# One block of a weight loaded ahead of k and v: a change of load order in a fused attention and MLP kernel

## Chip, cores, metric

The kernel runs on one NeuronCore of one Trainium2 chip. The metric is the device time of one execution in microseconds (us). Traces are of one execution each; "span" is from the first to the last instruction of the trace, 1.8 us less than the timed figure of the same execution. PE is TensorE (with its weight loads as PEld), DVE VectorE, ACT ScalarE, POOL GpSimd, SP SyncE; the results of the matmuls stand in tiles of PSUM pools, which DVE or ACT reads (in the trace of before ACT takes 1.02 us for each `rt<-hps`, DVE 0.76 us for two `qpTp<-tq`).

## The reference

Batch 8, 8 heads, 576 positions, head size 64, all in float32. Linear attention with cosine and sine features, then an MLP with a squared ReLU:

```python
k_p, q_p = phi(k, cos, sin), phi(q, cos, sin)   # relu(x) * cos, relu(x) * sin, side by side
kv  = einsum('bhsf,bhsd->bhfd', k_p, v);  z = k_p.sum(axis=2)
x   = (q_p @ kv) / ((q_p * z).sum(-1) + 1e-6)   # per head; reshaped to 4608 x 512
out = relu(x @ w_in)**2 @ w_out                 # w_in 512 x 2048, w_out 2048 x 512
```

## The kernel before

The weights are loaded once, cast to bf16 by the DMA, in four pieces each; a w_out block is four row groups of 128 rows (1 MB in float32; the page lists 512 KB for each of these loads). q, k and v are loaded per batch, as one main part and two tails. Batch 0 comes in on the SP queue. Everything here is issued by POOL (GpSimd):

```python
def load_w2(i, n):                       # block i of n of w_out
    h0, h1 = i * HB // n, (i + 1) * HB // n
    nc.gpsimd.dma_start(out=w2sb[:, h0:h1, :], in_=moe_w_out[h0 * P : h1 * P, :]...)

with tc.manual_schedule():
    load_batch(0, nc.sync, "kvq")
    ...                                  # constants, warm-up matmuls, features of k, v of batch 0
    for i in range(4):
        load_w1(i, 4)
    load_batch(1, nc.gpsimd, "qkv")      # the lines of the change
    for i in range(4):
        load_w2(i, 4)
    load_batch(2, nc.gpsimd, "qkv")
    att_kv(0, 0)
    ...                                  # attention of batch 0
    for s in range(len(slots)):
        run(s)
```

The work then goes through slots. Slots 0 to 7 are the first GEMM of batch 0, with parts of the attention of batches 0 and 1 between them; slots 8 to 15 are the second GEMM of batch 0. It is the first reader of w_out. It has four outputs at once: the two halves of one buffer of the PSUM pool `ps_h`, and the two buffers of `ps_y`. `ps_y` also holds the transposed q features:

```python
def gemm2(b, s):
    if b == 0:
        if s == 0:
            yh = ps_h.tile([P, 2, DM], F32, name="yh", tag="hps", bufs=2)
            ypss[b] = [yh[:, 0, :], yh[:, 1, :]]
            for i in range(2):
                yps = ps_y.tile([P, DM], F32, name="yps", tag="yps", bufs=2)
                ypss[b].append(yps[:, :])
        for hb in range(s * HB // 8, (s + 1) * HB // 8):     # two row groups per slot
            for tt in range(J):                              # four outputs
                gemm2_mm(b, tt, hb, ypss[b][tt])
```

The last transposes of q (`tq`, line 279) stand in slot 7 and are copied out by DVE (`qpTp`, line 288). The features of k and the copy of v of batch 1 stand in slots 8 and 9, and their product (`kz`, line 236) in slot 10.

## Time and profile before

Three runs took 300.75 to 301.13 us, median 301.09. Busy shares of the span: PE 97%, ACT 51%, DVE 46%, POOL 16%. PE (TensorE) is the engine to look at, and its only wait on w_out is the 1.27 us in front of the second GEMM of batch 0, the place that the change aims at. The lines for it are in the prediction.

### The profile page before, as it was taken

To read this page: it belongs to the slowest core of one execution; us is meant where nothing else is said; L and a number is where in the kernel's file an instruction comes from. 1 tells how busy PE (TensorE), PEld (TensorE's weight loads), DVE (VectorE), ACT (ScalarE), POOL (GpSimd) and SP (SyncE) were. 2 spreads that over 40 slices of the span, in tenths; PEclk is the share of its full clock that TensorE was granted. 3 is DMA by queue.
4 is the path that set the end of the run, shared out by engine and by line. 5 is a ranking of instruction groups with operands and counts; after the bars stand their busy time and mean duration, and the time that the engine had idled before them with its cause. 6 is when DMAs were issued, how large, how long until landed. Compare 5 with 4: busy or idle time off the path is not lost.

```text
span 299.0 us, 6477 instructions
## 1 busy us (share of the span) xinstructions
PE 291.1 (97%) x2701; PEld 202.3 (68%) x2701; DVE 136.6 (46%) x333; ACT 153.0 (51%) x213; POOL 47.8 (16%) x79
## 2 busy tenths in 40 slices
PE   8799989999999999999999999999999999999995
PEld 3379845889456984589654884589754894589544
DVE  2367654475648386228730287227740273024100
ACT  3465743666738554655554555555563552255311
POOL 1463404661121002000021001100021000100000
DMA  7999993999639987898568926898468115100021
GB/s 211 284 204 342 288 231 123 329 355 248 163 97 181 229 253 112 257 248 239 140 175 208 327 43 90 268 256 242 124 168 212 37 35 81 70 35 3 34 73 70
DMA packets 77069, 52.98 MB, mean 177 GB/s; under 512 B 52240, under 2 KB 71952, under 8 KB 77040
## 3 DMA queue, kind: packets, MB, share of 16 engines
q1 hardware_dynamic: 67120, 29.50, 42.2%
q0 software_dynamic: 9776, 22.94, 27.1%
q8 instruction: 21, 0.34, 0.5%
q10 hardware_dynamic: 144, 0.13, 0.1%
q14 instruction: 8, 0.07, 0.1%
HBM read 36.70 MB, written 9.44 MB: 154 GB/s over the span
## 4 chain that ended last, share of the span: by engine, by line
PE 86%; DMA 10%; POOL 1%; SPq 1%; issue 0%; ACT 0%; ACTq 0%
PE yps L413 40%; PE hps L378 38%; DMA q<-in_q_dram 5%; PE num L305 3%; DMA w2sb<-in_moe_w_out_dram 3%; DMA v<-in_v_dram 3%; PE kz L236 3%; PE yh L413 2%; POOL w1sb L117 1%; SPq L69 0%; PE tx L346 0%; PE tq L279 0%; POOL vt L69 0%; POOL vext L195 0%; SPq L64 0%
## 5 line engine op out<-in xcount | busy, mean ns | idle before, releaser
L378 PEld LDWEIGHTS <-w1sb 128*128 128x128 bf16 x1312 | 113.2, 98 | 12.1
L378 PE MATMUL hps<-xT,w1sb 128*128 128x256 bf16 (+1 forms) x1056 | 118.0, 269 | 0.0
L413 PE MATMUL yps<-w2sb,gT 128*128 128x512 bf16 (+1 forms) x496 | 110.4, 372 | 0.0
L386 ACT ACTIVATE rt<-hps 128x1024 bf16<-128x1024 f32 x72 | 73.7, 1024 | 59.2 <-DVE gT L393 32.8
L413 PEld LDWEIGHTS <-gT 128*128 128x128 bf16 x528 | 49.6, 98 | 54.0 <-DMA w2sb<-in_moe_w_out_dram 1.4
L393 DVE TENSOR_TENSOR gT<-rt 128x1024 bf16<-128x1024 bf16 x64 | 44.0, 688 | 82.8 <-ACT rt L386 82.8
L409 POOL DMA_DIRECT2D out_dram<-ysb x34 | 20.5, 605 | 176.2 <-ACT ysb L399 173.2
L399 ACT COPY ysb<-yps 128x512 f32<-128x512 f32 (+1 forms) x35 | 20.0, 575 | 55.3 <-PE yps L413 55.3
L181 ACT ACTIVATE qp<-q,sin_col 128x512 bf16<-128x512 f32 x32 | 21.9, 719 | 6.4 <-DMA q<-in_q_dram 6.4
L181 ACT ACTIVATE kp<-k,sin_col 128x512 bf16<-128x512 f32 x32 | 21.2, 714 | 3.1 <-DMA k<-in_k_dram 3.1
L319 DVE TENSOR_TENSOR x<-num,rden 128x512 bf16<-128x512 f32 x32 | 22.1, 691 | 1.1
L171 DVE TENSOR_SCALAR qp<-q,cos_col 128x512 bf16<-128x512 f32 x32 | 14.5, 492 | 11.7 <-DMA q<-in_q_dram 11.7
L315 DVE TENSOR_SCALAR den<-num 128x8 f32<-128x8 f32 (+1 forms) x40 | 6.6, 165 | 23.9 <-PE num L305 23.7
L171 DVE TENSOR_SCALAR kp<-k,cos_col 128x512 bf16<-128x512 f32 x32 | 15.1, 481 | 4.9 <-DMA k<-in_k_dram 4.9
L378 PE MATMUL hps<-xTt,w1sb 128*128 128x128 bf16 x256 | 15.3, 219 | 0.0
L413 PE MATMUL yps<-w2sb,gTt 128*128 128x512 bf16 x64 | 14.5, 379 | 0.0
L195 DVE CAST vext<-v 128x512 bf16<-128x512 f32 (+1 forms) x31 | 13.0, 425 | 2.9 <-DMA v<-in_v_dram 2.9
L305 PEld LDWEIGHTS <-qpT 128*128 128x128 bf16 (+1 forms) x240 | 10.3, 100 | 3.3 <-issue 1.7
L236 PEld LDWEIGHTS <-kp 128*128 128x128 bf16 x256 | 9.5, 97 | 4.4 <-issue 1.9
L201 PE MATMUL wm<-zeros 128*128 128x512 bf16 x42 | 10.9, 421 | 1.2 <-DVE zeros L86 1.2
L305 PE MATMUL num<-kvz,qpT 128*128 128x65 bf16 (+1 forms) x240 | 11.7, 194 | 0.0
L236 PE MATMUL kz<-vext,kp 128*128 128x65 bf16 x256 | 9.9, 193 | 1.6 <-DVE vext L195 1.6
(58 smaller groups left out, 132.6 us busy)
## 6 DMA issues: line engine op xcount, KB each, us to landing
out_dram<-ysb POOLq DMA_DIRECT2D x28, 256.0 KB, 3.9
k<-in_k_dram SPq DMA_DIRECT2D x5, 1024.0 KB, 6.2
v<-in_v_dram SPq DMA_DIRECT2D x5, 1024.0 KB, 6.7
q<-in_q_dram SPq DMA_DIRECT2D x5, 1024.0 KB, 5.9
q<-in_q_dram POOLq DMA_DIRECT2D x3, 1024.0 KB, 13.7
k<-in_k_dram POOLq DMA_DIRECT2D x3, 1024.0 KB, 10.1
v<-in_v_dram POOLq DMA_DIRECT2D x3, 1024.0 KB, 9.7
w1sb<-in_moe_w_in_dram POOLq DMA_DIRECT2D x4, 512.0 KB, 8.8
```

The lines of the kernel that those rows point to most:

```text
L171: nc.vector.tensor_scalar(out=dst[:, :, 0:D], in0=src, scalar1=0.0, scalar2=cos_col[:, j : j + 1], op0=ALU.max, op1=ALU.mult,)
L181: nc.scalar.activation(out=dst[:, :, D:F], in_=src, func=ACTF.Relu, scale=sin_col[:, j : j + 1])
L195: copy(out=vx[:, j, h0:h1, 0:D], in_=piece("v", b, j)[:, h0:h1, :])
L236: nc.tensor.matmul(out=kz[:, half, hh * E1 : (hh + 1) * E1], lhsT=lhsT, rhs=rhs, start=(j == 0 and hh == 0), stop=(j == J and hh == HH - 1),)
L305: nc.tensor.matmul(out=out, lhsT=lhsT, rhs=kvz[:, half * HH + hh, :], start=True, stop=True)
L319: nc.vector.tensor_tensor(out=x_of(b, j).rearrange("p (b k) (l d) -> p b k l d", b=n, l=2), in0=n4[:, :, :, 0:D].rearrange("p b (k l) d -> ...
L378: nc.tensor.matmul(out=out, lhsT=w1sb[:, kb, hb * P : (hb + 1) * P], rhs=rhs, start=(kb == 0), stop=(kb == KB - 1),)
L386: nc.scalar.activation(out=rt[:, :, :], in_=hps[:, :, :], func=ACTF.Relu)
L393: nc.vector.tensor_tensor(out=dst, in0=rt[:, :, :], in1=rt[:, :, :], op=ALU.mult)
L399: nc.scalar.copy(out=ysb[:, c0:c1], in_=acc)
L409: eng.dma_start(out=dst, in_=ysb[p0 : p0 + n, c0:c1])
L413: nc.tensor.matmul(out=acc, lhsT=lhsT, rhs=w2sb[:, hb, c0:c1], start=(hb == 0), stop=(hb == HB - 1))
```

## The change

The intent is to have the first block of w_out on the chip when PE first wants it, at the cost of k and v of batch 1, which are wanted later.

```diff
-        load_batch(1, nc.gpsimd, "qkv")
-        for i in range(4):
+        load_batch(1, nc.gpsimd, "q")
+        load_w2(0, 4)
+        load_batch(1, nc.gpsimd, "kv")
+        for i in range(1, 4):
             load_w2(i, 4)
```

## The prediction

> **What bounds the kernel now.** I read the page first, then the waits, the chain that ended last, and the order of time on each engine between 11 and 60 us. The page says that PE (TensorE) is the engine to look at:
>
> ```profile
> span 299.0 us, 6477 instructions
> PE 291.1 (97%) x2701; PEld 202.3 (68%) x2701; DVE 136.6 (46%) x333; ACT 153.0 (51%) x213; POOL 47.8 (16%) x79
> ```
>
> PE is idle for 299.0 - 291.1 = 7.9 us in the whole span. By the order of time on PE, 2.8 of it lie before 11.75 us, where the first matmuls on real data start, and 3.2 behind the last matmul at 295.8. A change in load order can win only what remains. The table of waits names that remainder; in each line the sum comes first, then how often, then the longest:
>
> ```profile
> PE kz L236 <- DVE vext L195: 1.6, 1, 1.6
> PEld L413 <- DMA w2sb<-in_moe_w_out_dram: 1.4, 1, 1.4
> PE yh L413 <- DMA w2sb<-in_moe_w_out_dram: 1.3, 1, 1.3
> ```
>
> The last two are one event, seen from the weight loads and from the matmuls. It is the only PE wait that involves w_out, and it happens once. The chain of waits shows where, and that PE works without a gap behind it:
>
> ```profile
> 14.87 13.74 DMA q<-in_q_dram
> 28.61 0.28 issue
> 28.89 0.61 POOL vt L69
> 29.50 8.73 DMA w2sb<-in_moe_w_out_dram
> 38.23 0.05 issue
> 38.27 0.60 PE yh L413 x2
> 38.88 0.43 PE yps L413 x2
> ```
>
> Columns: start, length, what. Block 0 of w_out is issued at 29.50 and lands at 38.23. From 38.27 until 295.78, just before the last copy, the chain is PE pieces alone. The order of time on PE gives the size:
>
> ```profile
> 36.40 0.61 PE L279 MATMUL tq<-ident,qp 128*128 128x128 bf16 x8
> 38.27 0.60 PE L413 MATMUL yh<-w2sb,gT 128*128 128x512 bf16 x2 [1.27 <-DMA w2sb<-in_moe_w_out_dram]
> ```
>
> PE ends the transposes at 37.01 (rounded; 38.27 - 1.27 = 37.00) and starts the second GEMM of batch 0 at 38.27. So 1.27 us, 0.4% of 301.09, is the ceiling of what this change can remove.
>
> [...] the loads issued on POOL (GpSimd) land in order of issue, q of batch 1 at 14.87 + 13.7 = 28.6, k at 17.27 + 15.1 = 32.4, v at 23.36 + 12.1 = 35.5, w_out block 0 at 38.2. [...]
>
> **The change, part by part.** Nothing is removed or added. The instruction lists of PE, DVE (VectorE), ACT (ScalarE) and SP are identical; on POOL the first w_out load moves up past six loads (k, two k tails, v, two v tails). Cost of issue: the same instructions, 0.76 us for a w_out block, 0.9 for a main load, 0.6 for a tail.
>
> *Issue waits.* POOL's order of time shows that it often waits before issuing:
>
> ```profile
> 20.84 0.62 POOL L69 DMA_DIRECT2D kt<-in_k_dram  x1 [2.02 <-DMA w1sb<-in_moe_w_in_dram]
> 23.36 0.90 POOL L64 DMA_DIRECT2D v<-in_v_dram  x1 [1.90 <-DMA w1sb<-in_moe_w_in_dram]
> 25.86 0.64 POOL L69 DMA_DIRECT2D vt<-in_v_dram  x1 [1.60 <-DMA w1sb<-in_moe_w_in_dram]
> 28.89 0.62 POOL L69 DMA_DIRECT2D vt<-in_v_dram  x1 [2.39 <-DMA q<-in_q_dram]
> ```
>
> The compiled list explains them: POOL's loads rotate through eight semaphores, so each waits for the load eight places earlier. The moved block becomes the eighth load and waits for nothing: it is issued behind the q tails, at 17.27 instead of 29.50. Each load of k and v inherits the wait of its new place: k at 18.0 (the first w_in piece lands at 11.73 + 6.1 = 17.8), its tails at 20.84 and 23.36, v at 25.86 and its tails at 28.6 and about 29.2. Block 1 goes out near 30, as now; block 2 waits for block 0, block 3 for k.
>
> *Landings.* Between v and block 0, and between blocks, the spacing is 38.2 - 35.5 = 2.7 and about 2.5 us (two issues starting at 29.50 and 30.26 have a median of 9.6 to landing; with 8.7 for the first, 10.5 for the second, so block 1 lands at 40.8). Block 0 should then land at 28.6 + 2.7 = 31.3, and k and v slip by one block, 2.5 us: k to 34.9, v to 38.0. Block 1 has the same bytes ahead of it as before and stays at 40.8; so do blocks 2 and 3. All are estimates from the trace's own spacings.
>
> *What k and v meet.* DVE and ACT don't take them up at once, as DVE's order of time shows:
>
> ```profile
> 37.04 0.76 DVE L288 COPY qpTp<-tq 128x512 bf16<-128x512 bf16 x2 [0.44 <-PE tq L279]
> 37.72 0.68 DVE L393 TENSOR_TENSOR gT<-rt 128x1024 bf16<-128x1024 bf16 x1
> 38.31 0.48 DVE L171 TENSOR_SCALAR kp<-k,cos_col 128x512 bf16<-128x512 f32 x1
> 38.71 0.42 DVE L195 CAST vext<-v 128x512 bf16<-128x512 f32 x1
> ...
> 41.50 0.30 DVE L193 CAST vextt<-vt 128x256 bf16<-128x256 f32 x1
> ```
>
> DVE first reads k at 38.31 (3.4 us after the new landing) and v at 38.71 (0.7 us after). ACT first reads k at 37.52. The reader on PE, the k-v product, runs at 43.46 now and near 42.5 when it moves up by 1 us; DVE has its last input ready at 41.80. That is 0.7 us of slack at its first matmul, more for v's tail, which only its last eight need. v may be about 0.7 + 0.7 = 1.4 us later than I estimate before PE stands still for it.
>
> *What PE gets.* Block 0 is in place 5.7 us before PE wants it, so PE starts at 37.01. Two smaller waits then come to light.
> First, the four outputs of that GEMM use two buffers each of two PSUM pools; the fourth takes the buffer of the transposes that PE has only just ended, which DVE copies out until 37.04 + 0.76 = 37.80. PE arrives at 37.01 + 3 x 0.216 = 37.66 (a pair of these matmuls takes 0.43). With the hand-over I count 0.2 us lost.
> Second, block 1 is first read after 16 matmuls. Three are done by then and 13 x 0.216 = 2.81 follow 37.85: PE is there at 40.66[...]. Before, it came at 41.90 (by the chain, 38.27 plus the first pieces), 1.1 us after block 1's landing; now it meets the landing at 40.8 almost exactly. Should block 1 land there, its matmuls start at 40.85.
> Sum: 41.90 - 40.85 = 1.05 us gained; I take off 0.1 for the chance that block 1 is a little later. Blocks 2 and 3 (issued by 35, needed near 46 and 50) land well ahead. All later work of the other engines follows PE's progress, and the DMA queue drains by about 49 us (18 GB/s between 47 and 50 us), so nothing should give the gain back. Predicted: 301.09 - 0.95 = 300.1 us.
>
> **Rivals.** *The wait moves to k and v.* They land later, and DVE works in order, so a late v would also hold its later k pieces. Needed for a loss: v at 39.4 or later. For it: the loads get their semaphores later (v's tail at 29.2 at the earliest). Against: the queue then still holds some 8 us of earlier bytes. If true, PE idles before the k-v product, by 0.5 to 2 us, and the time is 300.5 to 302.
> *The wait moves to block 1 of w_out.* Likely as a trace of a wait, since the times tie. If the reorder costs the queue 0.5 us, half the gain goes: 300.6. [...]
> *Everything is gained.* If the PSUM buffer is free in time and block 1 lands earlier, at 40.3: 1.2 us, 299.9.
> *Nothing is gained, since a later wait takes it back.* PE has no gap after 38.27 in the chain, but small slacks elsewhere may be used up. It would leave 301.1. I see no line that speaks for it.
>
> **Range and chances.** The three runs spread over 0.38 us, about a third of the effect. The gain can hardly exceed 1.27, and 0.3 is a plausible low; with 0.2 to 0.4 us of run-to-run shift, 299.5 to 300.8 should hold it 8 times in 10. Faster by 2% would need 6.0 us where 1.27 are to be had. Slower by 2% would need a 7 us stall; only a much later landing of v could do it.
>
> **What would show it.** Right: PE's wait on w_out at 37 us is gone or under 0.3; block 0 lands near 31, v near 38; a wait of 0.1 to 0.3 on the DVE copy in front of the fourth output; the k-v product of batch 1 starts near 42.5 without a wait on k, v or DVE; PE's idle time falls by about 1 us and its busy time stays at 291. Wrong: PE idle before the k-v product, a wait for block 1 over 0.4 us, or a new gap after 50 us.

41.90 - 40.85 = 1.05 us, less 0.1, gives the 0.95 us and the 300.1 us. The "8 us of earlier bytes" is an estimate from the 8.73 us that block 0, issued at 29.50, took to land. The eight semaphores are read from the compiled list; the four waits in its lines agree, each with the load eight places earlier (the last tail of v goes out at 28.89, after q of batch 1 has landed at 28.6).

## More of the kernel before

The granted clock is the share of its full speed that the profile records for PE, and a run's mean clock is its average over the span.

## The result, and the profile after

| | runs | median us | range us |
|---|---|---|---|
| before | 4 | 301.11 | 300.75 to 302.01 |
| changed | 4 | 299.52 | 299.38 to 299.65 |

The ratio is 0.9943, with an interval of 0.992 to 0.9965. (Ratios here are the mean time of one kernel's fast runs over that of the other's of the same rounds, so not quite the ratio of the medians.) The class "within 2%" was right. The gain was not: 1.6 us by the medians, 1.7 by the ratio, where 0.95 was predicted. The time lies on the lower edge of the stated range; by the ratio, 0.9943 x 301.09 = 299.4, it is outside.

The page of the changed kernel:

```profile
span 297.6 us, 6476 instructions
PE 292.3 (98%) x2701; PEld 202.5 (68%) x2701; DVE 136.5 (46%) x333; ACT 153.0 (51%) x213; POOL 47.8 (16%) x79
```

The span is 1.4 us shorter, yet PE is busy 1.2 us longer. That has nothing to do with the change: the 34 warm-up matmuls at the start took 8.96 us in the trace of before and 10.32 in this one, and a second trace of the kernel before also has 292.1. Busy time alone would mislead here.

PE's order of time, where the wait was (start, length, engine, line, what, count, idle before and its cause):

```profile
36.04 0.61 PE L279 MATMUL tq<-ident,qp 128*128 128x128 bf16 x8
36.49 0.59 PE L413 MATMUL yh<-w2sb,gT 128*128 128x512 bf16 x2
36.92 0.38 PE L413 MATMUL yps<-w2sb,gT 128*128 128x512 bf16 x1
37.50 0.39 PE L413 MATMUL yps<-w2sb,gT 128*128 128x512 bf16 x1 [0.20 <-DVE qpTp L288]
```

The wait on w_out is gone; the second GEMM starts as the transposes end, and the fourth matmul waits 0.20 us for the DVE copy that frees its buffer. DVE's order of time shows that copy, and that k and v are read without a wait:

```profile
36.69 0.76 DVE L288 COPY qpTp<-tq 128x512 bf16<-128x512 bf16 x2 [0.44 <-PE tq L279]
37.36 0.68 DVE L393 TENSOR_TENSOR gT<-rt 128x1024 bf16<-128x1024 bf16 x1
37.96 0.48 DVE L171 TENSOR_SCALAR kp<-k,cos_col 128x512 bf16<-128x512 f32 x1
38.35 0.42 DVE L195 CAST vext<-v 128x512 bf16<-128x512 f32 x1
```

The landings (issue on POOL plus time to landing, us):

| load | before: issued, landed | changed: issued, landed | predicted landing |
|---|---|---|---|
| q, batch 1 | 14.87, 28.6 | 14.52, 28.1 | 28.6 |
| w_out block 0 | 29.50, 38.2 | 16.91, 31.2 | 31.3 |
| k, batch 1 | 17.27, 32.4 | 17.66, 34.1 | 34.9 |
| v, batch 1 | 23.36, 35.5 | 25.37, 37.4 | 38.0 |
| w_out block 1 | 30.26, 40.8 | 29.64, 40.0 | 40.8 |

So where did 1.4 us of span come from? The fifth pair of `yh` matmuls, the first to read block 1, starts at 41.90 before and 40.48 after, 1.42 earlier (by the chain that ended last, as in the prediction; the order of time has both 0.17 earlier). Of this, 0.35 is older than the change: the trace of before has PE at the end of the transposes at 37.00, this one at 36.65, as all of it had begun earlier: q of *batch 0*, loaded by SP long before the moved load, was first used at 14.36 against 14.03. The other 1.07 is the removed wait less the new one, as predicted. In these two traces the mechanism gave its predicted size, and the timed runs showed 0.5 more.

### The profile page after: what moved, and what is told of

Same layout as the page of the kernel before. It is cut to its first block, busy times and chain, and to the rows that moved or that the text cites. A ratio compares the mean times of both kernels' runs of the same rounds, so it can differ in the third digit from the quotient of the medians.

```text
span 297.6 us, 6476 instructions
## 1 busy us (share of the span) xinstructions
PE 292.3 (98%) x2701; PEld 202.5 (68%) x2701; DVE 136.5 (46%) x333; ACT 153.0 (51%) x213; POOL 47.8 (16%) x79
## 3 DMA queue, kind: packets, MB, share of 16 engines
q1 hardware_dynamic: 67120, 29.50, 43.2%
## 4 chain that ended last, share of the span: by engine, by line
PE 93%; DMA 3%; SPq 1%; DVE 1%; ACT 0%; issue 0%; ACTq 0%
PE hps L378 43%; PE yps L413 40%; PE num L305 3%; DMA q<-in_q_dram 3%; PE kz L236 3%; PE yh L413 2%; PE tq L279 1%; SPq L69 1%; PE tx L346 1%; PE wm L209 1%; ACT qpTp L288 0%; SPq L64 0%; DVE qp L171 0%; DVE qpTp L288 0%; ACT ysb L399 0%
## 5 line engine op out<-in xcount | busy, mean ns | idle before, releaser
L201 PE MATMUL wm<-zeros 128*128 128x512 bf16 x42 | 12.2, 460 | 1.2 <-DVE zeros L86 1.2
L413 PEld LDWEIGHTS <-gTt 128*128 128x128 bf16 x64 | 6.3, 98 | 7.6
```

The source lines that it names most:

```text
L413: nc.tensor.matmul(out=acc, lhsT=lhsT, rhs=w2sb[:, hb, c0:c1], start=(hb == 0), stop=(hb == HB - 1))
```

## The experiments

Theory at first (A): the start varies from run to run, and the change is worth its 1.07 us. Rival (B): the changed program starts earlier as well, always. A third reading came out of the first session: (C) the wait itself is longer in most runs of the kernel before than in the trace that I read. Each session has its own chip; a session's first-named time of the kernel before is from runs taken between those of the tried kernels. By the 2% rule of the record all these kernels are "same", e8 "unclear"; the text goes by the ratios and their 95% intervals.

### Second session: the kernels again, and the 0.2 us wait

**e1**, the kernel before, unchanged.

> The kernel before, unchanged, as a control. Theory A (the extra 0.35 us at the start is run-to-run variation of the first loads): the first use of q of batch 0 on DVE, at 14.36 us in the first trace of this kernel, moves by some tenths between traces of one and the same kernel; PE waits 1.2 to 1.3 us for block 0 of w_out again; ratio to before 1.000 within 0.1%. Theory B (the start depends on the program): 14.3 to 14.4 us again, and 14.0 only in the changed kernel.

Measured: 301.3 us median of 6 (300.6 to 301.9), ratio 0.9999 (0.9973 to 1.0025). Its trace:

```profile
36.88 0.61 PE L279 MATMUL tq<-ident,qp 128*128 128x128 bf16 x8
39.38 0.60 PE L413 MATMUL yh<-w2sb,gT 128*128 128x512 bf16 x2 [1.89 <-DMA w2sb<-in_moe_w_out_dram]
```

The wait is 1.89 us, half as long again as in the first trace of the same program. The first use of q of batch 0 came at 14.88 (14.36 before): the start moves by half a microsecond in one program, which is enough for A to explain the 0.35. But I had expected the wait to stay at 1.2 to 1.3, and that failed.

**e2**, the changed kernel, unchanged.

> The changed kernel, unchanged. Theory A: the gain is only the wait for block 0 less the new 0.2 us wait, 1.07 us by the traces, so a ratio of 0.9964 and about 300.0 us where before takes 301.1. Theory B: the start is earlier with the changed program as well, 1.4 us, ratio 0.9953, with the first use of q at 14.0 us again. If the first ratio of 0.9943 (1.7 us) holds, more than the two terms that the traces show is in it and both theories lack something.

Measured: 299.81 us median of 6 (299.34 to 300.08) against 301.02 of 11 (300.45 to 302.9); ratio 0.9951 (0.9927 to 0.9974), 1.5 us. First use of q at 14.23. The fourth matmul waits 0.20 us again. The first matmul on block 1 starts at 40.62, 0.18 late, with block 1 landing at 40.6: the tie that the prediction saw, lost this time.

**e3**, the changed kernel with the first eight matmuls of the second GEMM in the order of outputs:

```diff
-        for hb in range(s * HB // 8, (s + 1) * HB // 8):
-            for tt in range(J):
-                gemm2_mm(b, tt, hb, ypss[b][tt])
+        hbs = range(s * HB // 8, (s + 1) * HB // 8)
+        if s == 0:
+            pairs = [(hb, tt) for tt in range(J) for hb in hbs]
+        else:
+            pairs = [(hb, tt) for hb in hbs for tt in range(J)]
+        for hb, tt in pairs:
+            gemm2_mm(b, tt, hb, ypss[b][tt])
```

> The changed kernel, with the first eight matmuls of the second GEMM of batch 0 ordered by output and not by row block, so that the fourth output (whose PSUM buffer DVE still copies out) is first written by the seventh matmul and not by the fourth. If the 0.2 us wait on the DVE copy is real: it is gone (PE is there 1.3 us after the start, the copy ends after 0.8), the whole 1.27 us are gained, 0.2 us (0.07%) faster than the changed kernel, unless block 1 of w_out (first read 0.3 us behind its landing in the changed kernel) becomes the wait. If the wait is made by the profile only: same time as the changed kernel.

Measured: 300.0 us median (299.19 to 300.4), ratio 0.9957 (0.9929 to 0.9984). In the trace the wait is gone, and from the start of the second GEMM (36.97) to the end of the last matmul (294.47) it is 257.50 us, where the changed kernel takes 294.36 - 36.49 = 257.87. So the wait costs 0.37 by the trace: 0.20 of idle time, and about 0.17 because the matmul in front of the wait lasts 0.38 us (36.92 in PE's order of time above), where in a row the next one follows after 0.216 (pairs start 0.43 apart). The times do not show it: the start of this trace's GEMM was 0.36 later than in e2, more than the reordering is worth. By the clock of whole runs this one is inconclusive.

**e4**, the same reordering in the kernel before.

> The same reordering of eight matmuls in the kernel before. The DVE copy ends at 37.80 us there, before block 0 lands at 38.23, so the reordering alone should do nothing: ratio 1.000, PE still waits 1.2 to 1.3 us for block 0. If instead it is faster by 0.2 us, the reordering helps for another reason than the wait on the copy.

Measured: 301.28 us median (300.74 to 303.86), ratio 1.0011 (0.9977 to 1.0046): nothing gained, as expected. Its trace gave the longest wait of all:

```profile
36.13 0.61 PE L279 MATMUL tq<-ident,qp 128*128 128x128 bf16 x8
38.96 1.04 PE L413 MATMUL yh<-w2sb,gT 128*128 128x512 bf16 x4 [2.22 <-DMA w2sb<-in_moe_w_out_dram]
```

What follows so far. In all three traces of the old load order the last matmul ends 257.5 us behind the start of the second GEMM (295.78 - 38.27, 296.89 - 39.38, 296.47 - 38.96). The end of the kernel before is thus *the landing of block 0 plus 257.5*, and that of the changed kernel *PE's arrival plus 257.9* (up to 258.05 if block 1 is late), counted there from the first matmul, which starts 0.16 before the transposes are through. The landing moved between 38.2 and 39.3, and PE's arrival between 36.7 and 37.5, not together. The mean wait of the three is (1.27 + 1.89 + 2.22) / 3 = 1.79. By the same arithmetic as in the prediction the gain is the wait less 0.2, less another 0.0 to 0.2 for block 1: 1.4 to 1.6, and e2 measured 1.5.

One thing did not fit: single runs of the old order at 302.39, 302.9 and (e4) 303.86, 1.3 to 2.8 us over the median of the other 20 (301.05). Just these three of its 23 runs on this chip have a mean granted clock of 0.994; all others have 0.998 or more. The third session shows what that is.

### Third session: more slip, and a longer wait on purpose

The kernel before took 300.41 us (300.33 to 300.8, 7 runs) on this chip. Traces of this and the next session lack 24 matmul records each (2677 where the others have 2701), so sums of PE's busy time over a whole trace are not read from them. **e5** and **e6** put two and three blocks ahead of k and v, **e7** puts block 0 between k and v, and **e8** is the kernel before with block 1 ahead of block 0:

```diff
 # e5; e6 with 3 for 2
+        load_batch(1, nc.gpsimd, "q")
+        for i in range(2):
+            load_w2(i, 4)
+        load_batch(1, nc.gpsimd, "kv")
+        for i in range(2, 4):
+            load_w2(i, 4)
 # e7
+        load_batch(1, nc.gpsimd, "qk")
+        load_w2(0, 4)
+        load_batch(1, nc.gpsimd, "v")
 # e8
         load_batch(1, nc.gpsimd, "qkv")
-        for i in range(4):
+        for i in (1, 0, 2, 3):
             load_w2(i, 4)
```

> Blocks 0 and 1 of w_out both ahead of k and v of batch 1, so v lands one block later still: 37.5 (mean of three traces of the changed order) + 2.6 = 40.1 us. My slack: DVE needs 3.1 us from v to the last input of the k-v product, so 43.2; PE would read it at 43.0. Expected: a PE wait of 0.2 to 0.3 us on DVE in or before the k-v product, no wait for block 1, and a time within 0.4 us of the changed kernel (about 299.9). Rival (k and v have much more slack than I think): no wait, 299.5. Rival (k and v are critical as soon as they slip): 1 to 2 us slower than the changed kernel.

Measured: 300.66 us median (299.84 to 300.82), ratio 1.0001 (0.9985 to 1.0016). All of the gain is lost, and my bound of 0.4 us over the changed order failed (that order was not run on this chip; e7 below, nearest to it, took 299.5). PE in e5:

```profile
43.25 0.40 PE L236 MATMUL kz<-vext,kp 128*128 128x65 bf16 x8 [0.32 <-DVE vext L195]
43.98 0.40 PE L236 MATMUL kz<-vext,kp 128*128 128x65 bf16 x8 [0.33 <-DVE vext L195]
```

v landed at 41.3, not 40.1. DVE stood 2.63 us for it and took the next piece of k only behind it, at 41.64. From there the count holds: 41.3 + 3.1 = 44.4 for the last input of the product, which PE would have read at 42.28 + 1.07 = 43.35 (the changed kernel reads it 1.07 us after the product's start), and the product took 2.47 us instead of 1.30. The slack was counted right and the landing 1.2 us too early.

> Three blocks ahead of k and v: v at 42.7 us, last input of the k-v product at 45.8, PE wants it at 43.0. Expected: a PE wait of about 2.8 us in front of or inside the k-v product of batch 1, and a time 2.8 us over the changed kernel, 302.6, so slower than the kernel before. If slack for v is larger by 1 us than I count, 301.6.

Measured: 301.61, 302.49, 303.78 and 304.31 us; ratio 1.0077 (1.0036 to 1.0119). The kernel is slower than before, so v is next in line once it slips by more than one block. The two slower runs have a clock of 0.994, the others 1.0 and 0.999; the two fast ones lie 2.1 and 3.0 us over e7, around the 2.8 expected.

> Block 0 behind q and k and ahead of v. By the three traces of the kernel before k lands at 32.9 us on average, so block 0 at 35.7, still ahead of PE's arrival at 36.7 to 37.5. Theory (only landing before PE's arrival counts): same time as the changed kernel, 299.8, no wait for block 0. If a slow stream of loads (they differ by 1 us between traces) makes block 0 late in some runs: up to 0.3 us slower on average. Rival (the gain comes from the other order of loads in the stream, not from the wait): between before and the changed kernel.

Measured: 299.5 us median (298.81 to 300.08), ratio 0.9967 (0.9949 to 0.9984), 1.0 us faster than before. Block 0 landed at 34.1 and PE did not wait for it. From the start of the second GEMM to the last matmul it takes 257.86 us, as in the changed kernel. So, as far as four runs and this trace tell, it matters only that the block lands before PE comes, not where it stands.

> The kernel before, with block 1 of w_out loaded ahead of block 0. If the end of the kernel before is set by the landing of block 0 alone (in three traces the last matmul ends 257.5 us behind the start of the second GEMM), block 0 lands one block later, 2.55 us, PE waits 1.8 + 2.55 = 4.3 us, and the time rises by 2.5 us to about 303.6. If something else bounds the kernel before, less: 301 to 302.

Measured: 305.72 us median (304.79 to 306.75), ratio 1.0175 (1.015 to 1.0201), 5.2 us slower where 2.5 were expected. Block 0 landed at 40.5 and PE waited 4.05 us, where 4.3 were expected. The rest is in what follows the wait. PE's order of time, then the table of stretches (columns: stretch, length, busy time of PE, PEld, DVE, ACT, POOL with instructions in brackets, granted PE clock, DMA share, GB/s):

```profile
40.56 0.39 PE L413 MATMUL yh<-w2sb,gT 128*128 128x512 bf16 x1 [4.05 <-DMA w2sb<-in_moe_w_out_dram]
41.01 0.59 PE L413 MATMUL yps<-w2sb,gT 128*128 128x512 bf16 x2
...
42.20 1.06 PE L413 MATMUL yps<-w2sb,gT 128*128 128x512 bf16 x2
```

```profile
42.00:43.00 1.00, 1.00 (x3) 0.30 (x2) 0.00 (x0) 0.00 (x0) 0.00 (x0) 0.50 1.26 210
43.00:44.00 1.00, 1.00 (x4) 0.40 (x3) 0.00 (x0) 0.00 (x0) 0.00 (x0) 0.50 1.18 290
44.00:45.00 1.00, 1.00 (x4) 0.36 (x3) 0.00 (x0) 0.00 (x0) 0.00 (x0) 0.53 1.09 398
45.00:46.00 1.00, 1.00 (x6) 0.46 (x5) 0.00 (x0) 0.00 (x0) 0.00 (x0) 1.00 0.98 392
```

A pair of matmuls takes 0.85 us from start to start instead of 0.43: about a microsecond after work resumed, PE went to half its clock, and stayed there for some 3.4 us (41.5 to 44.9, by the clock shares of 0.88 from 40 to 42 us and 0.53 from 44 to 45). From the start of the second GEMM to the last matmul it is 259.2 us, not 257.5, so one such stretch costs 1.7 us and brings the mean clock of the run to 0.994. Two of the four runs have 0.994 (304.79, 305.61) and two 0.989 (305.83, 306.75), which would be two stretches; only the first is traced.

The trace of e6 has such a stretch too, without one long gap in front of it (columns as above):

```profile
42.00:43.00 1.00, 0.34 (x2) 0.07 (x1) 0.06 (x1) 0.42 (x2) 0.00 (x0) 1.00 1.22 216
43.00:44.00 1.00, 0.40 (x8) 0.37 (x8) 1.00 (x3) 0.00 (x0) 0.00 (x0) 1.00 1.22 261
...
45.00:46.00 1.00, 0.67 (x16) 0.64 (x14) 1.00 (x4) 0.00 (x0) 0.00 (x0) 0.83 1.06 423
46.00:47.00 1.00, 0.67 (x13) 0.54 (x12) 0.03 (x1) 0.41 (x1) 0.00 (x0) 0.50 0.40 160
```

The longest gap was 1.08 us and PE was busy 0.34 to 0.67 of each microsecond from 42 to 47 us; the clock fell to 0.50 at about 45.7 us (0.83 from 45 to 46) and was back at about 49.1 (0.96 from 49 to 50). The longer waits of e1 (1.89 us) and e4 (2.22 us) cost no such stretch: those traced runs have mean clocks of 0.999 and 1.0. So in these traces the length of the longest gap does not tell whether clock is lost. What does, and why only some runs of one program lose clock, was not shown.

### Fourth session: the wait filled, and a closing comparison

**e9** is e8 with 14 matmuls on zeros in the gap, behind the transposes of slot 7:

```diff
+    at(7, fill, 14)
```

> Block 1 loaded ahead of block 0 as before, but with 14 matmuls on zeros (3.0 us at 0.216) put into PE's wait of 4 us; they write a PSUM buffer that nobody reads, the result stays right. Theory (a PE that idles for some us gets half the clock for some us after, as the trace without the filling showed: 0.50 from 42 to 44.5 us, mean 0.994 or 0.989): the clock stays at 0.998 to 1.0 and the time falls by 1.5 to 3 us, to the landing of block 0 alone, 2.55 us over the kernel before. Rival (the low clock is the run's state and has nothing to do with the wait): still 0.99 and about 5 us over the kernel before.

Measured: 303.31 us median of 5 (302.89 to 304.1) against 300.76 of 11; ratio 1.0092 (1.0074 to 1.0109), 2.7 us. The five clocks are 0.998 to 1.0:

```profile
36.72 2.97 PE L209 MATMUL wm<-zeros,ident 128*128 128x512 bf16 x13
40.37 0.61 PE L413 MATMUL yh<-w2sb,gT 128*128 128x512 bf16 x2 [0.68 <-DMA w2sb<-in_moe_w_out_dram]
```

The landing of block 0 sets nearly the same start of the GEMM (40.37 against 40.56), the rest takes 257.5 us again, and of the 5.2 us that e8 lay over its kernel before, 2.5 are gone although PE has more to do. So the low clock is caused by the wait, and the rest is the one block's delay that e8 was to show (2.55 expected). e8 and e9 ran on different chips, but on neither had the kernel before a run with such a clock.

**e10**, the kernel before, and **e11**, the changed one, on the same chip. (The "3 of 17" in e10's expectation is a slip: 3 of 23, the third being e4's.)

> The kernel before once more, on the chip of the other three. Its profile gives one more wait for block 0 (1.27, 1.89, 2.22 us so far), and its runs the share with a clock of 0.994 and 1.5 us or more over the rest (3 of 17 on one chip, 0 of 7 on another). Ratio 1.000 to before.

Measured: 300.68 us median of 6 (300.32 to 301.04), ratio 1.0002 (0.9987 to 1.0017), no run with a clock under 0.999. The trace is of the slowest of the six (301.04):

```profile
36.34 0.61 PE L279 MATMUL tq<-ident,qp 128*128 128x128 bf16 x8
38.51 0.39 PE L413 MATMUL yh<-w2sb,gT 128*128 128x512 bf16 x1 [1.56 <-DMA w2sb<-in_moe_w_out_dram]
```

> The changed kernel on the same chip. Theory: time before less (mean wait for block 0 less 0.2 to 0.4), so 1.0 to 1.7 us faster (ratio 0.9945 to 0.9967), with no run at a clock under 0.998 and a spread under 1 us.

Measured: 299.72 us median of 6 (299.45 to 300.22), ratio 0.9972 (0.9956 to 0.9988): 0.9 us, under the 1.0 to 1.7 that I expected, and just the 0.95 of the prediction. The profiled runs differ by more, 301.04 - 299.65 = 1.39, and there the wait was 1.56: the arithmetic "wait less 0.2" holds for the pair (1.36).

**e12**, e7 with the reordering of e3, as the best version that the experiments point to:

> Best guess: block 0 behind k of batch 1, and the first eight matmuls of the second GEMM ordered by output so that the fourth output's buffer is free in time. By the traces of the reordering alone the time from the start of that GEMM to the last matmul is 257.50 us against 257.87 in the changed kernel, so 0.37 us faster than the changed kernel, 0.2 of it lost again if block 1 of w_out is late. In the first try the times did not show it; the start of a run moves by as much.

Measured: 299.33 us median of 6 (299.11 to 300.6), ratio 0.9965 (0.9947 to 0.9984). By its trace, 257.68 us from the start of the second GEMM to the last matmul against 257.87 in e11: 0.2 better, as expected where block 1 is late. By the times it is not set apart from the changed kernel, since the intervals overlap.

## Why the prediction was right or wrong

**Right: what bounds the kernel, and what the change touches.** In the traces PE's wait for block 0 was the only thing to gain, the chain behind it held (nothing was given back), and k and v did no harm.

**Right: the landings.** The loads landed in order of issue again, block 0 at 31.2 (31.3 predicted); k, v and block 1 came 0.6 to 0.8 us earlier than predicted, 0.35 of which is that trace's earlier start. The three landings did not keep their sum: block 0, k and v landed at 106.1 us in sum before and at 102.7 after, 1.05 of the difference being the earlier start, and the prediction's own three estimates add up to 104.2.

**Right: the two small waits.** The copy of the transposes cost 0.20 us in each trace of the changed kernel; block 1 was a tie, won in the first trace and lost by 0.18 in e2. From PE's arrival to the first matmul on block 1 it took 40.48 - 36.65 = 3.83 us, where the prediction's figures give 40.85 - 37.01 = 3.84. That they meet is partly luck: the 3.84 has a wait for block 1 in it, without which they give 40.66 - 37.01 = 3.65, and the first trace had no such wait. What it had instead is the 0.17 beyond the idle time (0.37 in e3 less the wait of 0.20), which the prediction's sum does not count. That the outputs take "two buffers each of two PSUM pools" was a misreading (see the code above) without effect, for the fourth output does take the buffer of the last transposes.

**Right, and not foreseen as close: the slack of v.** One block of slip is free, two cost all of the gain (e5), three cost 2 to 5 us (e6). By an estimate from e5's trace a loss begins when v lands later than about 43.35 - 3.1 = 40.2 us; the prediction had 39.4.

**Wrong: the step "So 1.27 us, 0.4% of 301.09, is the ceiling of what this change can remove."** It takes the wait of one execution for that of the kernel. The wait is a difference of two times, the landing of block 0 and PE's arrival. Four traces of the old order gave 1.27, 1.89, 2.22 and 1.56 us, mean 1.74, and I had read the shortest. With the mean, the sum of the prediction, wait less 0.2 and less about 0.1, gives 1.4. There was a hint: the profiled run took 300.79 us, 0.3 less than the median of its group. The waits of the timed runs of the first comparison are not known, since only one of its runs of the kernel before was traced; that they were longer is inferred from the later traces. Chance is a rival for a part of the excess: with four runs a side the interval of the first ratio (0.992 to 0.9965) overlaps that of e11 (0.9956 to 0.9988), where the gain was the predicted one.

**Wrong: a term was missing from that sum.** A wait of PE can also cost clock behind it (e8: 4.05 us of wait, then half clock for 3.4 us). In the second session three of 23 runs of the old order carry the mark of it, a mean clock of 0.994 and about 1.7 us; on the two other chips none of 7 and none of 17. Of the runs without that wait only e6's had it (two of four, with gaps before the product), and 0 of 32 of the changed order, e3, e7 and e12. That e8's waits cause the mark and e9's filling removes it was shown; that the three unprofiled runs had the same cause is inferred from their clocks. In the first comparison one run of before took 302.01 us; its clock was not recorded. Without it the gain of means is 301.0 - 299.5 = 1.5, with it 1.7.

**Theories.** B, in which the changed order starts earlier *always*, fell: the first use of q of batch 0 came at 14.36, 14.88 and 14.43 in the kernel before, and at 14.03, 14.23 and 13.98 in the changed one. These do not overlap, but e4, e8 and e9, with block 0 behind k and v, had 14.16, 14.01 and 14.01, and e3, e5, e6, e7 and e12, with a block moved forward, 14.35, 14.33, 14.18, 13.56 and 14.09. The means of all traces, 14.31 and 14.09, lie 0.2 apart at a spread of 0.3, so a small shift is not excluded. A alone was not enough, for it had left the wait at 1.27. C carries the result: the gain is the run's wait, less 0.2 to 0.4, and now and then a stretch at half clock.

**What stays open.** The gain was 1.7, 1.5, 1.0 (e7) and 0.9 us in four sessions; how much of that is chance and how much the chip was not settled. The traces show that from POOL's first w_in issue to the landing of block 0 it takes 26.5, 27.1, 27.5 and 26.7 us in four traces of the same order, a spread of 1 us, as large as the whole predicted gain. From that issue to PE's arrival it takes 25.3 us in each of the four (37.00 - 11.73, 37.49 - 12.22, 36.74 - 11.47, 36.95 - 11.69). So the early or late start moves both alike, and the whole variation of the wait arises in the stream of loads. Why this stream is slower on one chip or in one run was not tested.

## What to carry to other kernels

The wait on a DMA was here the difference of two times that move from run to run (1.27 to 2.22 us in four traces of one load order), so its length in one trace is a sample, not a ceiling; compare the profiled run with the median of the timed ones, and take several traces before sizing a gain of this kind. Once block 0 landed before its reader came, moving it further forward bought nothing (257.86 us from the second GEMM to the end in e7, 257.87 in the changed kernel), and a second block ahead of k and v made v so late that all of the gain was lost (e5). And a gap on PE, or several short ones close together, may cost more than its length: behind 4.05 us in e8, and behind gaps of at most 1.08 us in e6, the granted clock was 0.50 for some 3.4 us, which cost 1.7 us in e8. So look at the mean clock of every run, and at the stretches behind the gap.
